# Seven products instead of eight for the last group of layer 2, and its h in a row ahead of y

## The chip, the cores and the metric

The kernel runs on one core of one Trainium2 chip. The metric is the device time of one execution in microseconds (us); the median of three runs stands for a kernel. A difference of about 0.2% of this kernel's time is what a measurement can tell from no change. The engines are TensorE (PE; its weight loads are PEld), VectorE (DVE), ScalarE (ACT), GpSimd (POOL), and SyncE (SP), which here only issues DMAs.

## What is computed

Random-feature attention and, on its result, two feed-forward layers without a bias, all in fp32 precision:

```python
x = attention(q, k, v, omega)        # reshaped to 2304 tokens x 512
h = x @ moe_w_in                     # 512 -> 2048
g = h - tanh(h)
x = g @ moe_w_out                    # 2048 -> 512
h = x @ moe2_w_in                    # layer 2, same sizes
g = h * (1.0 / (1.0 + exp(-1.702 * h)))
out = g @ moe2_w_out
```

TensorE multiplies fp32r numbers. Each operand is split into a rounded part (hi) and the rest (lo), and a product of two blocks is made as three matmuls (`PASSES`: hi hi, hi lo, lo hi), so that one block product of 128 x 128 weights by 384 tokens is three matmuls of 384 columns.

## The kernel before

Only layer 2 is touched. Its 2304 tokens are three blocks (`sb`) of 768, each of two halves of 384 (`TW`). Its 2048 features are eight pairs `j` of two 128-feature tiles. A group `n` is a pair of (block, j); there are `NG` = 24 groups, numbered 0 to 23. The first 16 belong to the blocks 0 and 1; groups 16 to 23 are the third block, with the pairs of `LAST` in order, so that group 23 has pair 2.

**h.** For a group h is a 2 x 2 block product (two feature tiles by two token halves), and it is made Strassen-Winograd fashion from seven products P1 to P7 instead of eight (`h_prod`, L906; each six matmuls, L916). They run in the order of `SLOTS` (P1, P7, P6, P4, P5, P2, P3), one in each of the seven slots `s` of a group's turn; the P2 in slot 5 is the next group's. P1, P6, P5, P3 add up in one PSUM bank (`a`), P7 and P4 in another (`c`), P2 in a third (`b`). Between the products other engines read the running sums and add them: `vec` (L1069 on) does in slot 0 `h_add` G11 (VectorE, reads bank a), in slot 1 the activation of G11 and the copy `s7` of bank c (ScalarE), in slot 2 the copy `s2` of bank a, in slot 3 `gsplit` of G11 and then `h_add` G21, in slot 4 the activation of G21 and `h_add` G22 (reads bank a), in slot 5 the activation of G22, in slot 6 `gsplit` of G21 and the activation of G12. So P6 may not write bank a until `h_add` G11 has read it, P5 not until `s2` has, and P3 not until `h_add` G22 has.

`gsplit` (L1027 on) makes the two parts of a g: a cast on ScalarE (L1035) and a subtraction (L1036), which is GpSimd's. The buffer for G21 (tag `g10`) exists once, those for G11 and G22 twice.

**y.** For groups 16 to 22 (`YG` <= n < `YE`, told by `yform`) y is made from seven products as well (`y_prod`, L984; `y_add`, L997). They need sums of w_out (`wfs`, loaded into `wos`) and the differences T1 to T4 of the g, which `forms` makes during the next group's turn: subtractions on GpSimd (L1040), then a cast on ScalarE (L1044) and a subtraction on GpSimd (L1045). The products write two PSUM tiles of two banks in turn; after each, VectorE adds the tile to an SBUF sum `yacc` (128 x 768, L997) before the next product writes that tile. Their order is `YP` (P3, P1, P2, P6, P7, P5, P4): in slots 1 to 6 of group n+1's turn stand P1 to P4 of group n, in slot 0 of the turn after that its P3. So h products of one group and y products of the one before it alternate on TensorE.

Group 23 is different: after the loop over its h, a last turn (n = 24) runs group 22's P3 and then eight plain chunks (`y_chunk`, L937, six matmuls each into one of four banks, 48 in all), each followed by a VectorE addition of 128 x 384 (L955; the last in two halves, L951) and a store.

The sums of w_out for the pairs 0 and 1 are made from the weights in SBUF at groups 2 and 3 (`late_ticks`), those for the pairs 3 to 7 when these weights are prepared. Pair 2 has none.

Each engine works off its instructions in the order in which the program issues them. Stores go through a list `later`, which `flush` issues on SP at the start of the next slot. All other DMAs of layer 2 are SP's too: in slot 0 of a group's turn stand the loads of the next group's w_in sums (`win`, in two pieces), of this group's w_out (`wout`) and, up to group 22, of its sums (`wos`).

Of the kernel before, what the change touches and what calls it, by code (L numbers as in the profile page):

```python
# [61 lines left out]
YG, YE = 2 * NPAIR, 3 * NPAIR - 1  # L62
YP = ("P3", "P1", "P2", "P6", "P7", "P5", "P4")
WID = dict(P1=0, P2=1, P7=2, P6=3, P5=4, P3=5, P4=6)
# [3 lines left out]
def body(ctx, tc, qT, kT, v, om, w1, w2, out):  # L68
# [393 lines left out]
    def out_sums(s, f1, f2):  # L462
        a11, a21, a12, a22 = f1[:, :256], f1[:, 256:], f2[:, :256], f2[:, 256:]
        for o, x, y, op in (
                (s[:, 0, :], a21, a22, ALU.add), (s[:, 2, :], a11, a21, ALU.subtract),
                (s[:, 1, :], s[:, 0, :], a11, ALU.subtract), (s[:, 3, :], a12, s[:, 1, :], ALU.subtract)):
            nc.gpsimd.tensor_tensor(out=o, in0=x, in1=y, op=op)

    def out_split(q, i, s, t):
        v = t.rearrange("p (a h c) -> p a h c", h=2, c=256)  # L470
        two(v[:, :, 0, :], v[:, :, 1, :], s[:, i:i + 2, :], nc.gpsimd)
        store(wfs[q, :, i * 512:(i + 2) * 512].rearrange("p (a h c) -> p a h c", h=2, c=256), v.bitcast(F32))


    def late_ticks(q):
        st = {}

        def whole():
            w = st["w"] = cv.tile([128, 2, 512], F32, tag="raw", name="wsum", bufs=2)
            nc.vector.tensor_tensor(  # L480
                out=w, in0=wout[q][:, :, 0, :].bitcast(F32), in1=wout[q][:, :, 1, :].bitcast(F32), op=ALU.add)

        def sums():
            st["s"] = ssum_tile((128, 4, 256))
            out_sums(st["s"], st["w"][:, 0, :], st["w"][:, 1, :])

        def part(i):
            out_split(q, i, st["s"], cv.tile([128, 2 * 512], F32R, tag="ye", name="stg", bufs=2))

        return [whole, sums, lambda: part(0), lambda: part(2)]  # L490

# [439 lines left out]
    def y_chunk(n, t, d):  # L931
        sb, j = GROUPS[n]
        yb = pt("hs" if n < NG - 1 else ("y2", "y0", "y3", "y1")[d])
        dst, k = yb[:, :TW], 0
        for f in range(2):
            for a, c in PASSES:
                nc.tensor.matmul(  # L937
                    dst, wout[j][:, f, a, d * 128:d * 128 + 128], gt[n, f, t][:, c, :], start=(k == 0), stop=(k == 5))
                k += 1
        first, last = (0, NPAIR - 1) if sb < 2 else (LAST[0], LAST[-1])  # L940
        if j == first and d % 2 == 0:
            yacc[sb, t, d // 2] = ya_tile("yacc")
        u = yacc[sb, t, d // 2][:, d % 2, :]
        if j == first:
            nc.vector.tensor_copy(out=u, in_=dst)
            return
        t0 = (2 * sb + t) * TW
        if n == NG - 1 and t == 1 and d == 3:
            for c, eng in ((0, nc.sync), (TW // 2, nc.scalar)):
                w = slice(c, c + TW // 2)  # L950
                nc.vector.tensor_tensor(out=u[:, w], in0=dst[:, w], in1=u[:, w], op=ALU.add)  # L951
                later.append((now[0], lambda eng=eng, w=w: eng.dma_start(
                    out=out[d, :, t0 + w.start:t0 + w.stop], in_=u[:, w])))
            return
        nc.vector.tensor_tensor(out=u, in0=dst, in1=u, op=ALU.add)  # L955
        if j == last:
            store(out[d, :, t0:t0 + TW], u)
# [14 lines left out]
    def y_prod(n, name):  # L972
        sb, j = GROUPS[n]
        i = "c" if name in ("P2", "P7", "P4") else "a"
        if name in ("P1", "P2", "P7"):
            ybank[n, i] = psb.tile([128, 2, 512], F32, tag="ya" if (i == "a") == (n % 2 == 0) else "yc", name="yb", bufs=1)
        dst = ybank[n, i]
# [4 lines left out]
        for d in range(2):  # L982
            for k, (a, c) in enumerate(PASSES):
                nc.tensor.matmul(  # L984
                    dst[:, d, :TW], w(a)[:, d * 128:d * 128 + 128], g[:, c, :],
                    start=(name in ("P1", "P2", "P7") and k == 0), stop=(k == 2), skip_group_check=True)

    def y_add(n, name):
        sb, j = GROUPS[n]
        src = ybank[n, "c" if name in ("P2", "P7", "P4") else "a"][:, :, :TW]  # L990
        h, t = dict(P1=(0, 0), P2=(0, 0), P3=(0, 1), P4=(1, 0), P5=(1, 1), P6=(1, 0), P7=(1, 1))[name]
        if n == YG and name in ("P1", "P6", "P7", "P3"):
# [4 lines left out]
        nc.vector.tensor_tensor(out=u, in0=src, in1=u, op=ALU.add)  # L997
# [29 lines left out]
    def gsplit(n, i):  # L1027
# [8 lines left out]
        nc.gpsimd.tensor_tensor(out=u[:, 1, :], in0=g, in1=u[:, 0, :].bitcast(F32), op=ALU.subtract)  # L1036
# [64 lines left out]

    do_y()
# [28 lines left out]
    for n in range(NG + 1):  # L1131
        sb, j = GROUPS[min(n, NG - 1)]
        for s in range(7):
# [6 lines left out]
            if n < NG or s < 2:  # L1140
                vec(n, s)
# [7 lines left out]
            if yform(m):  # L1149
                y_prod(m, YP[s])  # L1150
            if n == NG and s == 6:
                y_chunk(n - 1, 1, 3)
            if yform(m):
                y_add(m, YP[s])
                if m == YE - 1 and s == 0:
                    banks.close()
# [21 lines left out]
            q = n * 7 + s  # L1178
            if q in (16, 21):
# [33 lines left out]
            if n == 14:  # L1213
                if s == 0:
                    new_x2(2, 0)
                if SLOTS[s] != "P2":
                    new_x2(2, XID[SLOTS[s]])
    flush()
    assert not xticks and not later
# [46 lines left out]
```

## Time and profile before

| | us |
|---|---|
| median of 3 runs (lowest, highest) | 887.84 (887.63, 888.36) |
| the profiled execution | 888.12 |
| its span, first to last instruction | 886.0 |

| engine | busy us | share of the span | instructions |
|---|---|---|---|
| TensorE, matmuls | 880.8 | 99% | 5116 |
| VectorE | 617.5 | 70% | 956 |
| ScalarE | 582.6 | 66% | 1226 |
| GpSimd | 536.5 | 61% | 437 |

The chain that ended last is TensorE's to 99%. Times in the rows are us from the start of the span. A matmul's printed duration contains the time in which it drains; the distance of two starts tells what it costs in a row. In the stretch at the end of the kernel, the h products have L916, the seven-product y L984, the plain chunks L937.

### The profile page before, as it was taken

To read this page: it belongs to the slowest core of one execution; us is meant where nothing else is said; L and a number is where in the kernel's file an instruction comes from. 1 tells how busy PE (TensorE), PEld (TensorE's weight loads), DVE (VectorE), ACT (ScalarE), POOL (GpSimd) and SP (SyncE) were. 2 spreads that over 40 slices of the span, in tenths; PEclk is the share of its full clock that TensorE was granted. 3 is DMA by queue.
4 is the path that set the end of the run, shared out by engine and by line. 5 is a ranking of instruction groups with operands and counts; after the bars stand their busy time and mean duration, and the time that the engine had idled before them with its cause. 6 is when DMAs were issued, how large, how long until landed. Compare 5 with 4: busy or idle time off the path is not lost.

```text
span 886.0 us, 14390 instructions
## 1 busy us (share of the span) xinstructions
PE 880.8 (99%) x5116; PEld 806.2 (91%) x5116; DVE 617.5 (70%) x956; ACT 582.6 (66%) x1226; POOL 536.5 (61%) x437
## 2 busy tenths in 40 slices
PE   9999999999999999999999999999999999999998
PEld 7999988888898888888898899999999999999998
DVE  5889988766666655887777466477877775655555
ACT  7999988787777766777766645446565554544442
POOL 4555525656656565776866556537657565677774
PEclk9999999999999999999999999999999999999999
DMA  7888775033253341686471650824564224476752
GB/s 251 247 267 264 252 218 157 37 132 131 91 199 123 116 143 55 208 292 226 139 269 37 232 195 21 289 102 160 202 206 153 82 72 154 154 311 237 297 226 72
DMA packets 56071, 155.48 MB, mean 175 GB/s; under 512 B 6080, under 2 KB 12992, under 8 KB 52800
## 3 DMA queue, kind: packets, MB, share of 16 engines
q1 hardware_dynamic: 55712, 154.14, 50.3%
q8 instruction: 40, 0.66, 0.3%
q10 hardware_dynamic: 288, 0.43, 0.1%
q14 instruction: 31, 0.25, 0.1%
HBM read 106.32 MB, written 48.23 MB: 174 GB/s over the span
## 4 chain that ended last, share of the span: by engine, by line
PE 99%; ACT 1%; DVE 0%; issue 0%; DVEq 0%
PE y L418 22%; PE hs L380 22%; PE y L916 19%; PE hs L937 15%; PE yb L984 6%; PE y L220 3%; PE y L198 3%; PE y L134 2%; PE hs L165 2%; PE y L250 1%; PE y L937 1%; PE hs L916 1%; PE hs L168 1%; ACT kp L185 1%; PE y L216 1%; PE y L195 0%
## 5 line engine op out<-in xcount | busy, mean ns | idle before, releaser
L380 PE MATMUL hs<-xb,w 128*128 128x512 f32 (+1 forms) x960 | 209.1, 368 | 0.0
L380 PEld LDWEIGHTS hs<-xb,w 128*128 128x128 f32 x960 | 167.5, 189 | 30.0
L916 PE MATMUL y<-x,win 128*128 128x384 f32 x966 | 193.1, 334 | 0.0
L418 PE MATMUL y<-ghi,w 128*128 128x512 f32 (+1 forms) x640 | 192.4, 368 | 0.0
L394 POOL TENSOR_TENSOR glo<-wq,ghi 128x512 fp32r<-128x512 f32 x72 | 100.5, 1396 | 136.6 <-ACT ghi L392 135.0
L916 PEld LDWEIGHTS y<-x,win 128*128 128x128 f32 x966 | 169.8, 188 | 0.0
L410 DVE COPY_PREDICATED wq<-m,t 128x512 f32<-128x512 uint16 x72 | 88.5, 1230 | 104.6 <-POOL wq L408 102.8
L937 PE MATMUL hs<-g,wout 128*128 128x384 f32 x768 | 151.1, 334 | 0.0
L418 PEld LDWEIGHTS y<-ghi,w 128*128 128x128 f32 x640 | 116.6, 188 | 20.4 <-ACT ghi L392 0.4
L937 PEld LDWEIGHTS hs<-g,wout 128*128 128x128 f32 x768 | 134.8, 188 | 0.0
L418 PE MATMUL y<-glo,w 128*128 128x512 f32 (+1 forms) x320 | 117.8, 368 | 0.0
L1036 POOL TENSOR_TENSOR g<-sg,g 128x384 fp32r<-128x384 f32 x82 | 95.0, 1165 | 33.7 <-ACT g L1035 23.2
L408 POOL TENSOR_TENSOR wq<-wq,s 128x512 f32<-128x512 f32 x70 | 90.6, 1294 | 19.1 <-DVE wq L407 19.1
L955 DVE TENSOR_TENSOR yacc<-hs,yacc 128x384 f32<-128x384 f32 x112 | 61.4, 552 | 50.6 <-PE hs L937 49.8
L145 POOL PARTITION_ALL_REDUCE mq<-pq x32 | 62.6, 2002 | 53.0 <-ACT pq L143 53.0
L400 ACT ACTIVATE s<-hs 128x512 f32<-128x512 f32 x72 | 42.9, 596 | 60.0 <-PE hs L380 59.0
L418 PEld LDWEIGHTS y<-glo,w 128*128 128x128 f32 x320 | 60.3, 189 | 9.9
L997 DVE TENSOR_TENSOR yacc<-yb,yacc 128x768 f32<-128x768 f32 x45 | 43.1, 958 | 36.7 <-PE yb L984 36.5
L392 ACT CAST ghi<-wq 128x512 fp32r<-128x512 f32 x72 | 44.3, 615 | 29.1 <-DVE wq L410 29.0
L1023 ACT ACTIVATE sg<-y 128x384 f32<-128x384 f32 x55 | 27.0, 491 | 53.7 <-DVE y L1008 50.3
L331 DVE SCALAR_TENSOR_TENSOR raw<-raw 128x512 int32<-128x512 int32 x57 | 56.7, 995 | 2.0
L407 DVE SCALAR_TENSOR_TENSOR wq<-wq,hs 128x512 f32<-128x512 f32 x72 | 49.1, 682 | 12.6 <-ACT t L402 12.4
(153 smaller groups left out, 1518.0 us busy)
## 6 DMA issues: line engine op xcount, KB each, us to landing
raw<-w SPq DMA_DIRECT2D x57, 512.0 KB, 4.7
xb<-xs SPq DMA_DIRECT2D x24, 512.0 KB, 6.6
win<-wfi SPq DMA_DIRECT2D x9, 1280.0 KB, 6.8
wout<-wfo SPq DMA_DIRECT2D x9, 1024.0 KB, 8.3
wos<-wfs SPq DMA_DIRECT2D x7, 1024.0 KB, 8.8
xs<-xhl SPq DMA_DIRECT2D x12, 576.0 KB, 3.3
vt<-v SPq DMA_DIRECT2D x16, 325.0 KB, 4.2
wfs<-raw SPq DMA_DIRECT2D x10, 512.0 KB, 2.6
```

The lines of the kernel that those rows point to most:

```text
L145: nc.gpsimd.partition_all_reduce(mqs[i, j], pq[:, j * S:j * S + S], channels=128, reduce_op=bass.bass_isa.ReduceOp.max)
L331: nc.vector.scalar_tensor_tensor(out=c, in0=c, scalar=3, in1=z, op0=ALU.logical_shift_left, op1=ALU.bitwise_or)
L380: nc.tensor.matmul(h[:, j * n:j * n + n], w[:, 0, a, kt * 128:kt * 128 + 128], x[:, c, kt, :n], start=(k == 0), stop=(k == 11))
L394: nc.gpsimd.tensor_tensor(out=lo, in0=g, in1=hi.bitcast(F32), op=ALU.subtract)
L408: (nc.vector if si < 2 else nc.gpsimd).tensor_tensor(out=w, in0=w, in1=s, op=ALU.mult)
L410: nc.vector.copy_predicated(out=w, mask=m.bitcast(mybir.dt.uint16), data=t)
L418: nc.tensor.matmul(y[d][:, :n], w[:, 1, a, d * 128:d * 128 + 128], g[c][:, j * n:j * n + n], start=(first and j == 0 and k == 0), stop=(la ...
L916: nc.tensor.matmul(dst, w[:, WID[name], a, kt * 128:kt * 128 + 128], xt[:, kt, c, :], start=(first and k == 0), stop=(k == 5), skip_group_ ...
L937: nc.tensor.matmul(dst, wout[j][:, f, a, d * 128:d * 128 + 128], gt[n, f, t][:, c, :], start=(k == 0), stop=(k == 5))
L955: nc.vector.tensor_tensor(out=u, in0=dst, in1=u, op=ALU.add)
L984: nc.tensor.matmul(dst[:, d, :TW], w(a)[:, d * 128:d * 128 + 128], g[:, c, :], start=(name in ("P1", "P2", "P7") and k == 0), stop=(k == 2 ...
L1036: nc.gpsimd.tensor_tensor(out=u[:, 1, :], in0=g, in1=u[:, 0, :].bitcast(F32), op=ALU.subtract)
```

## The change

Group 23 makes y from seven products too (`YE` = 24), so `y_chunk` loses its special cases for the last group. Five things follow.

1. In group 23's turn the y products of group 22 are taken out (`LATE`), except P1 in slot 5; group 21's P3 stays in slot 0. So TensorE's order is: h P1, y P3 of 21, h P7, P6, P4, P5, y P1 of 22, h P3. In the last turn follow group 22's P2, P6, P7, P5, P4, P3 and group 23's P1; after the loop group 23's P2, P6, P7, P5, P4 and P3, the last in two halves by `d`, one VectorE addition for each and the very last in two halves of 192.
2. `vec` also runs in slots 0 to 5 of the last turn, for the forms of group 23.
3. In `gsplit` the subtraction for G11 and G21 of group 23 is VectorE's.
4. Group 23's products P1, P6, P5, P3 write the two h banks y0 and y2, with one VectorE addition of 128 x 384 for each; the others write one of the two tiles of the groups before, with an addition of 128 x 768. Stores go out after P2 and P4 (384 KB) and after P5 and P3 (192 KB and less).
5. The sums of w_out for pair 2 are made in groups 18 and 19 (`third_ticks`): two loads of 512 KB from DRAM in group 18's slot 0, two additions of 512 columns on VectorE in slots 5 and 6, four of 256 columns in group 19's slots 0 and 2, and in its slots 4 and 6 a cast on ScalarE, a subtraction on VectorE and a store of 512 KB. `load_wos` then runs for group 23 too.

```diff
-YG, YE = 2 * NPAIR, 3 * NPAIR - 1
+YG, YE = 2 * NPAIR, 3 * NPAIR
+LATE = {(NG - 1, s): (NG - 2, "P1" if s == 5 else None) for s in range(1, 7)}
+LATE.update({(NG, s): (NG - 2, (YP[2:] + YP[:1])[s]) for s in range(6)})
+LATE[NG, 6] = NG - 1, "P1"
...
+    def third_ticks(q):
...
+        def load():
+            for f in range(2):
+                t = st[f] = cv.tile([128, 2, 512], F32, tag="raw", name="wsum", bufs=2)
+                nc.sync.dma_start(out=t, in_=wfo[q, :, f * 1024:(f + 1) * 1024].rearrange("p (h c) -> p h c", h=2))
...
+        def whole(f):
...
+            nc.vector.tensor_tensor(out=st["w"][:, f, :], in0=st[f][:, 0, :], in1=st[f][:, 1, :], op=ALU.add)
...
+            out_sums(st["s"], st["w"][:, 0, :], st["w"][:, 1, :], nc.vector, part)
...
+            out_split(q, i, st["s"], cv.tile([128, 2 * 512], F32R, tag="ye", name="stg", bufs=2), nc.vector)
+
+        return {0: load, 5: lambda: whole(0), 6: lambda: whole(1), 7: lambda: sums(0), 9: lambda: sums(1),
+                11: lambda: part(0), 13: lambda: part(2)}
...
-    def y_prod(n, name):
+    def y_prod(n, name, ds=(0, 1)):
...
+            if n == NG - 1 and i == "a":
+                ybank[n, i] = [pt(f"y{2 * d}")[:, :TW] for d in range(2)]
...
+        for d in ds:
+            ends = (0, TW // 2, TW) if name == "P3" and d else (0, TW)
+            for a, b in zip(ends, ends[1:]):
+                nc.vector.tensor_tensor(out=u[:, d, a:b], in0=src[d][:, a:b], in1=u[:, d, a:b], op=ALU.add)
...
         nc.scalar.copy(out=u[:, 0, :], in_=g)
-        nc.gpsimd.tensor_tensor(out=u[:, 1, :], in0=g, in1=u[:, 0, :].bitcast(F32), op=ALU.subtract)
+        (nc.vector if n == NG - 1 and not t else nc.gpsimd).tensor_tensor(
+            out=u[:, 1, :], in0=g, in1=u[:, 0, :].bitcast(F32), op=ALU.subtract)
...
-            if n < NG or s < 2:
+            if n < NG or s < 6:
                 vec(n, s)
...
+            m, name = LATE.get((n, s), (m, YP[s]))
+            if name and yform(m):
+                y_prod(m, name)
+                y_add(m, name)
...
+    for name in YP[2:] + YP[:1]:
+        for ds in ((0,), (1,)) if name == "P3" else ((0, 1),):
+            flush()
+            y_prod(NG - 1, name, ds)
+            y_add(NG - 1, name, ds)
     flush()
+    banks.close()
```

## Rows read from the trace of the kernel before

**Rows 1.** The page: busy time, share of the span and instructions of each engine.
```profile
PE 880.8 (99%) x5116; PEld 806.2 (91%) x5116; DVE 617.5 (70%) x956; ACT 582.6 (66%) x1226; POOL 536.5 (61%) x437
```
**Rows 2.** The chain that ended last, its end: start us, us, what.
```profile
874.17 8.34 PE y L937 x48
...
882.53 0.36 DVE yacc L951
```
**Rows 3.** Windows: stretch, busy us (instructions) by engine, granted clock, DMA share, GB/s.
```profile
0.00:5.00 5.00, 3.50 (x8) 1.78 (x8) 0.80 (x4) 1.28 (x1) 0.19 (x4) 1.00 0.59 202
...
801.20:815.76 14.56, 14.56 (x86) 14.56 (x86) 8.39 (x10) 6.32 (x14) 10.90 (x12) 1.00 0.69 271
...
859.43:874.01 14.58, 14.58 (x86) 14.56 (x85) 9.24 (x11) 6.76 (x15) 11.12 (x13) 1.00 0.19 73
```
**Rows 4.** Timeline of TensorE, group 23's h P1 and P7: start us, us, engine, line.
```profile
859.43 1.20 PE L916 MATMUL y<-x,win 128*128 128x384 f32 x6
...
861.51 1.20 PE L916 MATMUL y<-x,win 128*128 128x384 f32 x6
```
**Rows 5.** Timeline of SP: the load of a group's w_out sums.
```profile
788.91 0.32 SPq L967 DMA_DIRECT2D wos<-wfs  x1
```
**Rows 6.** DMA issues, 780 to 886 us: KB each, median us to landing.
```profile
wos<-wfs SPq DMA_DIRECT2D x5, 1024.0 KB, 8.9
...
out<-yacc SPq DMA_DIRECT2D x7, 192.0 KB, 1.9
```
**Rows 7.** VectorE's groups by form: shapes, count, busy us, mean ns, idle before.
```profile
L460 DVE TENSOR_TENSOR wout<-raw,wout 128x512 fp32r<-128x512 f32 x10 | 8.6, 858 | 0.0
...
L480 DVE TENSOR_TENSOR wsum<-wout 128x1024 f32<-128x1024 f32 x2 | 2.8, 1382 | 0.0
```
**Rows 8.** Timeline of VectorE in group 23's turn: a y addition, an h_add.
```profile
861.71 0.96 DVE L997 TENSOR_TENSOR yacc<-yb,yacc 128x768 f32<-128x768 f32 x1 [0.40 <-PE yb L984]
...
868.99 0.56 DVE L1008 TENSOR_TENSOR hx<-y,s 128x384 f32<-128x384 f32 x1
```
**Rows 9.** The chain at the kernel's start: start us, us, what.
```profile
0.96 0.50 DVE warm L101
1.50 3.03 PE y L628 x4
```
**Rows 10.** Timeline of GpSimd in group 23's turn: T2's split, T3, T3's split.
```profile
863.72 1.01 POOL L1045 TENSOR_TENSOR fT<-T,fT 128x384 fp32r<-128x384 f32 x1 [2.13 <-ACT fT L1044]
864.70 1.01 POOL L1040 TENSOR_TENSOR T<-sg,sgb 128x384 f32<-128x384 f32 x1
866.33 1.02 POOL L1045 TENSOR_TENSOR fT<-T,fT 128x384 fp32r<-128x384 f32 x1 [0.62 <-ACT fT L1044]
```
**Rows 11.** Timeline of ScalarE in group 23's turn: the casts of T3 and G11.
```profile
865.74 0.51 ACT L1044 CAST fT<-T 128x384 fp32r<-128x384 f32 x1 [0.42 <-POOL T L1040]
866.15 0.51 ACT L1035 CAST g<-sg 128x384 fp32r<-128x384 f32 x1
```
**Rows 12.** Tile xi: VectorE's SBUF subtractions, duration ns min/median/max, first and last start.
```profile
L460 DVE TENSOR_TENSOR x<-xi,x x21: 543/552/1353, 452.6 to 763.6; 128x384 fp32r<-128x384 f32 x21
```
**Rows 13.** Timeline of VectorE, 747 to 758 us: subtractions between SBUF operands.
```profile
747.79 0.94 DVE L609 TENSOR_TENSOR xi<-xi 128x384 f32<-128x384 f32 x1
...
752.42 0.55 DVE L460 TENSOR_TENSOR x<-xi,x 128x384 fp32r<-128x384 f32 x1
752.89 0.55 DVE L609 TENSOR_TENSOR xi<-xi 128x384 f32<-128x384 f32 x1
...
757.46 0.90 DVE L460 TENSOR_TENSOR x<-xi,x 128x384 fp32r<-128x384 f32 x1
```
**Rows 14.** Timeline of GpSimd in the same stretch.
```profile
747.30 1.02 POOL L460 TENSOR_TENSOR x<-xi,x 128x384 fp32r<-128x384 f32 x1 [1.13 <-ACT x L459]
...
757.91 1.32 POOL L460 TENSOR_TENSOR x<-xi,x 128x384 fp32r<-128x384 f32 x1
```
**Rows 15.** The page's costliest groups: GpSimd's splits of g, mean ns of one.
```profile
L1036 POOL TENSOR_TENSOR g<-sg,g 128x384 fp32r<-128x384 f32 x82 | 95.0, 1165 | 33.7 <-ACT g L1035 23.2 <-issue 7.9 <-PE hs L937 1.4
```

## What the change was predicted to do

> **What bounds the kernel now.** I read the shares and the chain first. TensorE is busy for 880.8 of the 886.0 us span [rows 1], and the end of the chain is 48 matmuls without a gap and one VectorE addition behind them [rows 2]. By stage, a group in the row of seven-product groups and the last stretch of h both have TensorE busy in all of their time, at a granted clock of 1.00, that is 2.4 GHz [rows 3]. So fewer matmuls save time only if none starts to wait; the busy shares of the other engines matter only through the moment at which each answers TensorE. That has to be read in the order of the last 25 us. The profiled execution took 888.12 us for its span of 886.0; the median of the runs is 887.84. I work out a difference on the span and add it to the median.
>
> **What the change removes.** A product is six 384-column matmuls and takes 1.04 us from start to start (two from 859.43 to 861.51 [rows 4]); the printed 1.20 contains 0.16 of drain. Group 23's 48 y matmuls become 7 products of 6, that is 42: **-1.04 us**. On GpSimd three splits of group 23 go (G11 and G21 to VectorE, G12 altogether), and eight forms and splits come; they sit beside other work unless a product waits for them, see below.
>
> **What it adds in the third block.** In groups 18 and 19: two 512 KB loads, two 512-column sums, four 256-column sums and two 512-column subtractions on VectorE, two casts on ScalarE, two 512 KB stores. A group's loads are issued within some 3.5 us, the last at 788.91 for the group that starts at 786.64 [rows 5], and this one lands 8.9 us later [rows 6], in a group of 14.56 us [rows 3]; the 1 MB more is moved in the idle rest. The stores wait on SP ahead of group 20's load of w_in, which is due five slots later. From like instructions (1.38 us for two sums of 512 at once, 0.86 for a subtraction, and 0.69 as half of the 1.38 for each sum of 256 as a bound [rows 7]) VectorE gets some 5.9 us in two groups, each of which uses 8.39 of 14.56 us there [rows 3]. A y product's bank is needed again three products (3.12 us) after its end and its addition takes 0.20 + 0.96 [rows 8], so 1.9 us are spare; no single tick is longer than that. I take **0**; if GpSimd holds each of them up, two additions come late, and it costs up to 0.6 by my estimate from these spares.
>
> **What it moves: the row of h.** Group 23's P1, P7, P6, P4, P5 now stand with only group 21's P3 (after P1) and group 22's P1 (after P5) between them, and P3 follows. P3 accumulates into the bank that h_add G22 reads, so it waits for VectorE. I follow the queues, each instruction starting when its engine is free and its operand there, with the hand-overs of the rows: a product's last 1.04 us plus 0.20 to VectorE or ScalarE (860.48 + 1.04 to 861.71 [rows 8]), and 0.04 from VectorE to TensorE (0.96 + 0.50 to 1.50 [rows 9]).
> P1 starts at 859.43, P3 of group 21 1.04 later and P7 at 861.51, as before [rows 4]; P6, P4, P5 and group 22's P1 follow at 1.04 each, and TensorE is ready for P3 at 866.71. After P7 ScalarE casts T2, GpSimd splits T2 at 863.72 and forms T3 until 865.71 [rows 10]; ScalarE's next instructions are the cast of T3 (865.74) and, behind it, the cast of G11 (866.15 to 866.67) [rows 11]. None of these moves, because they hang on P7 and on GpSimd's order. But before, the split of G11 was GpSimd's, and VectorE was free for h_add G21 and G22. Now the subtraction stands on VectorE **ahead** of both. It starts at 866.70, while GpSimd splits T3 (866.33 to 867.35 [rows 10]).
> Such a subtraction takes 0.55 us at the median, at most 1.35 [rows 12]. A VectorE instruction on SBUF operands that started inside a GpSimd instruction took 0.94 us and ended 0.41 after it (748.73 against 748.32); beside none it took 0.55 [rows 13, 14]. So G11 ends at 867.35 + 0.41 = 867.76.
> The two h_adds follow (0.56 each [rows 8], the second 0.47 behind the first, as the pair at 752.42 and 752.89 in [rows 13]), each starting 0.09 before the last ends, as such a pair does: G22 ends at 868.71, and P3 starts at 868.75. **+2.04 us** (1.60 with a subtraction of 0.55, 2.4 with one of 1.35).
> The Trainium skill ("SBUF — State Buffer", section "SBUF: two separate sides") says that a VectorE operation with two SBUF inputs and a GpSimd operation exclude each other, the later one fully blocked. Taken to the letter, by an estimate, the whole 0.55 us would follow GpSimd's end, 0.14 more than rows 13 and 14 have, and the sum below would be 0.28 higher; the rows decide.
>
> **The first y product that is late.** G21 of group 23 goes into the one buffer that group 22's P2 reads, and P2 now follows P3: it ends at 870.83. The cast starts 0.20 later and ends at 871.54. The subtraction behind it meets GpSimd again. GpSimd's split of T1 began under G11's subtraction; an instruction in that place took 1.32 and ended 0.87 after VectorE's (757.91 under 757.46 [rows 13, 14]), so it ends at 868.63; then T4, its cast and its split bring the split of group 22's G22 to 871.21, and it ends at 872.23. So the subtraction of G21 ends at 872.64. Behind it stands the addition of P2: 872.55 to 873.51. P7 starts the same bank anew and waits for it until 873.55, while P6 has ended at 871.87: **+1.68 us** (1.20 with both subtractions at 0.55, 2.0 with both at 1.35).
>
> **The rest of the row of y.** With no h between, a bank is needed 1.04 us after its product's end, and the answer takes 0.20 + 0.96 + 0.04 = 1.20. One stall of 0.16 pays for two products; following the banks, it falls on P4 of group 22 and on P2, P7 and P4 of group 23: **+0.64**. At the end VectorE's last addition starts not 0.17 us behind TensorE's last matmul (882.36 without its drain, 882.53 [rows 2]) but behind P4's addition and a half of P3's: 0.20 + 0.87 + 0.47 - 1.04 = 0.50, **+0.33**. The last two 96 KB stores now follow 384 and 192 KB instead of 192 every 1.04 us; a 192 KB store lands in 1.9 us [rows 6] and nothing shows such a pile, so I take 0, up to 0.5. GpSimd's chain for group 23 (T1 from 872.2, T4's split done near 882.4) is ahead of P4, which starts near 883.6, by 1.2 us.
>
> **Sum.** -1.04 + 2.04 + 1.68 + 0.64 + 0.33 = +3.65 us: 887.84 + 3.65 = **891.5** (in the profiled execution 888.12 + 3.65 = 891.8). With the lower bounds, 1.60 and 1.20, it is +2.7 (890.5); with every upper one, 2.4 and 2.0 and 0.6 and 0.5, it is +5.4 (893.3).
>
> **Rivals.**
> *A, no conflict on SBUF.* Both subtractions take 0.55: the lower bounds above, 890.5. For it: the median row; against: GpSimd is at work almost without a break when each starts.
> *B, the queues answer in time.* If VectorE were done with h_add G22 before group 22's P1 ends (866.71), and with the addition of P2 before P6 ends, only the small stalls would stay: 887.84 - 1.04 + 0.64 + 0.33 = 887.8, not slower. It decides at one point, whether the cast of G11 stands behind T3's on ScalarE as it does now [rows 11]; the program's order leaves that, so T3 would have to come 2 us earlier, and GpSimd waits for P7 there. Little speaks for it.
> *C, GpSimd becomes the bound.* Its 384-column instructions took 1.02 in this stretch [rows 10] but 1.165 at the mean of the whole run [rows 15]. Ten of groups 22 and 23 at 0.15 more bring T4's split 1.5 us later, beyond the 1.2 that it has, and the h row's GpSimd steps 0.3: 0.3 to 1.1 more, 892.3.
> *D, the clock.* The granted clock is 1.00 in each row, also in the first 5 us, where TensorE idled for 1.5 us [rows 3, 9]; no row has a longer stop. If one of 2.04 us brought the level of 1.2 GHz, thirteen products would take 2.08 instead of 1.04: +13.5, near 905. The Trainium skill ("TensorE: Matmul & The Clock Gate", "Part 1: The HAM clock gate") tells of such a fall to half after idling; no run here shows one so far.
>
> **Chances.** Forecast 0.62, A 0.14, B 0.12, C 0.09, D 0.03. A difference of 0.2% (1.8 us) is about what a measurement of this kernel can tell from no change; slower by that begins at 889.6. Forecast, A, C and D are slower, 0.88; I take 0.05 off for stalls that come out below A's: slower 0.83, within 0.2% 0.14, faster 0.03 (B with more saved than the matmuls). The range leaves out B and D; it reaches from 0.6 below A, since each hand-over is read from one row, to the upper sum: **889.9 to 893.3**.
>
> **What would show it.** In the profile of the changed kernel: TensorE's waits, of which before has almost none, should name h_add G22 (about 2.0 us, once) and the addition of group 22's P2 (about 1.7, once), then four of about 0.16; the subtraction of G11 on VectorE should take about 1.06 us; groups 18 to 20 should keep 14.56 us each. The forecast is wrong if P3 of h starts within a few tenths of group 22's P1, if TensorE's waits name GpSimd's splits, or if the groups of the third block grow.

## The result

The changed kernel takes 893.9 us at the median of six runs (892.4 to 894.25), the kernel before 888.09 beside it (six runs, 887.63 to 888.37): a ratio of 1.006, 95% interval 1.0049 to 1.0071. It is slower, by 5.8 us, and lies above the predicted range. The profiled execution took 893.73 for its span of 891.9; before it was 888.12 for 886.0. So 5.90 us went into the span (and 0.29 less lay outside it), where the prediction had 3.65.

The page of after answers [rows 1]: VectorE and GpSimd work somewhat more, TensorE still fills 99%.

```profile
span 891.9 us, 14413 instructions
PE 882.2 (99%) x5110; PEld 805.5 (90%) x5110; DVE 626.5 (70%) x969; ACT 585.3 (66%) x1231; POOL 544.2 (61%) x442
```

TensorE's timeline from group 23's h P1 on (start, us, then engine, line, shapes; in brackets the idle time before and its releaser; h products have L943 now, y products L1009). Before, 22 products or chunks stood here 1.04 us apart [rows 2, 4].

```profile
860.18 1.20 PE L943 MATMUL y<-x,win 128*128 128x384 f32 x6
861.23 1.20 PE L1009 MATMUL yb<-g,wos 128*128 128x384 f32 x6
862.26 4.32 PE L943 MATMUL y<-x,win 128*128 128x384 f32 x24
866.42 1.20 PE L1009 MATMUL yb<-g,wout 128*128 128x384 f32 x6
869.48 1.31 PE L943 MATMUL y<-x,win 128*128 128x384 f32 x6 [1.85 <-DVE hx L1047]
870.62 1.20 PE L1009 MATMUL yb<-g,wout 128*128 128x384 f32 x6
871.66 1.20 PE L1009 MATMUL yb<-fT,wos 128*128 128x384 f32 x6
874.36 2.35 PE L1009 MATMUL yb<-fT,wos 128*128 128x384 f32 x12 [1.49 <-DVE yacc L1025]
876.80 1.28 PE L1009 MATMUL yb<-fT,wout 128*128 128x384 f32 x6
877.92 1.24 PE L1009 MATMUL yb<-g,wos 128*128 128x384 f32 x6
879.00 1.21 PE L1009 MATMUL y<-g,wout 128*128 128x384 f32 x6
880.30 1.28 PE L1009 MATMUL yb<-g,wout 128*128 128x384 f32 x6
881.42 1.21 PE L1009 MATMUL y<-fT,wos 128*128 128x384 f32 x6
...
886.26 1.21 PE L1009 MATMUL y<-g,wos 128*128 128x384 f32 x6
```

Two long gaps stand out, with the two releasers that the prediction named. TensorE is ready for h P3 at 866.42 + 1.04 = 867.46 and starts it at 869.48, 2.02 us later (bracketed as 1.85, since the row before is drawn with its drain); it is ready for P7 at 872.70 and starts it at 874.36, 1.66 later. Behind them a product comes after 1.04 us no more: two take 2.44 (874.36 to 876.80), then the steps are 1.12, 1.08, 1.30, 1.12, and on to the end 1.30 and 1.12 in turn.

VectorE's timeline over the first gap answers [rows 8], GpSimd's [rows 10]:

```profile
867.51 0.98 DVE L1075 TENSOR_TENSOR g<-sg,g 128x384 fp32r<-128x384 f32 x1 [4.09 <-ACT g L1074]
868.41 0.55 DVE L1047 TENSOR_TENSOR y<-y,s 128x384 f32<-128x384 f32 x1
868.88 0.54 DVE L1047 TENSOR_TENSOR hx<-y,s 128x384 f32<-128x384 f32 x1
```
```profile
867.07 2.27 POOL L1085 TENSOR_TENSOR fT<-T,fT 128x384 fp32r<-128x384 f32 x2 [0.62 <-ACT fT L1084]
```

The subtraction of G11 begins inside T3's split, takes 0.98 instead of 0.55, and both h_adds stand behind it. The end of the span shows in the chain (start, us, what):

```profile
885.14 1.29 PE yb L1009 x6
886.43 0.02 issue
886.46 0.96 DVE yacc L1025
887.41 0.47 DVE yacc L1032
887.88 0.26 DVEq L1309
```

The 5.90 us of the span then come from four places.

| stretch | before | after | difference |
|---|---|---|---|
| start of the span to group 23's h P1 | 859.43 | 860.18 | +0.75 |
| h P1 to the end of TensorE's last matmul, without drain | 22.93 | 27.12 | +4.19 |
| from there to the start of VectorE's addition for the last half product (before: the last chunk) | 0.17 | 0.49 | +0.32 |
| from there to the end of the span (the last stores) | 3.47 | 4.11 | +0.64 |

The 4.19 are 21 products instead of 22 (-1.04), less 0.05 that before lost too, plus 2.02, plus 1.66, plus 0.10 for h P3 (1.14 instead of 1.04), plus 1.50 for the unsteady steps behind. The first line, +0.75, is no effect of the change: it arises in the kernel's first 8 us, which the change does not touch. The chain at the start answers [rows 9], first before, then after:

```profile
4.53 0.43 PE hs L161 x2
4.96 1.62 PE y L165 x16
```
```profile
4.53 0.71 PE hs L164 x2
5.25 2.06 PE y L168 x16
```

In the fourteen traces of this case the 16 matmuls took from 1.14 to 2.06 us, whatever the edit (1.14 and 2.01 in two kernels that differ only from group 22 on, 2.06 also in the first experiment, where group 23 is as before); so below a kernel is measured by "h P1 to TensorE's end" (22.93 before, 27.12 after), which this start does not enter.

### The profile page after: what moved, and what is told of

The parts are those of the page before. It is cut to its first block, busy times and chain, and to the rows that moved or that the text cites. A ratio compares the mean times of both kernels' runs of the same rounds, so it can differ in the third digit from the quotient of the medians.

```text
span 891.9 us, 14413 instructions
## 1 busy us (share of the span) xinstructions
PE 882.2 (99%) x5110; PEld 805.5 (90%) x5110; DVE 626.5 (70%) x969; ACT 585.3 (66%) x1231; POOL 544.2 (61%) x442
## 4 chain that ended last, share of the span: by engine, by line
PE 97%; ACT 1%; DVE 1%; POOL 1%; issue 0%; DVEq 0%; POOLq 0%; ACTq 0%
PE y L421 22%; PE hs L383 22%; PE y L943 18%; PE hs L964 15%; PE yb L1009 6%; PE y L223 3%; PE y L201 3%; PE y L137 2%; PE hs L168 2%; PE y L253 1%; PE hs L943 1%; PE hs L171 1%; ACT kp L188 1%; PE y L219 0%; PE y L198 0%
## 5 line engine op out<-in xcount | busy, mean ns | idle before, releaser
L943 PE MATMUL y<-x,win 128*128 128x384 f32 x966 | 192.8, 334 | 1.8 <-DVE hx L1047 1.8
L943 PEld LDWEIGHTS y<-x,win 128*128 128x128 f32 x966 | 169.7, 188 | 2.2 <-DVE hx L1047 2.2
L1075 POOL TENSOR_TENSOR g<-sg,g 128x384 fp32r<-128x384 f32 x79 | 92.4, 1177 | 34.0 <-ACT g L1074 24.0
L1025 DVE TENSOR_TENSOR yacc<-yb,yacc 128x768 f32<-128x768 f32 x48 | 45.8, 955 | 29.4 <-PE yb L1009 29.2
```

The lines of the kernel that those rows point to most:

```text
L943: nc.tensor.matmul(dst, w[:, WID[name], a, kt * 128:kt * 128 + 128], xt[:, kt, c, :], start=(first and k == 0), stop=(k == 5), skip_group_ ...
L1075: (nc.vector if n == NG - 1 and not t else nc.gpsimd).tensor_tensor(out=u[:, 1, :], in0=g, in1=u[:, 0, :].bitcast(F32), op=ALU.subtract)
```

## The experiments

Theory: the moved subtractions stand on VectorE ahead of what TensorE waits for; the rest is small waits of VectorE's round trip. Rivals: the third block costs something; GpSimd is the bound in any order; the clock; the last stores. Each kernel has 5 to 11 runs. Ratios are to the kernel before, run beside it (medians of 888.27, 888.35 and 888.58 us in the three sets).

### Is it the third block?

Before, with the third block's sums made and stored, and read by nobody (`third_ticks` added, `YE` left as it was).

```diff
+            if n == NG - 6 and s == 0:
+                t3 = third_ticks(LAST[-1])
+            if 0 <= q - 7 * (NG - 6) in t3:
+                t3[q - 7 * (NG - 6)]()
```

> The kernel before with one part of the change alone: the sums of w_out for pair 2 are made in groups 18 and 19 and stored, and nobody reads them; group 23 stays as it was. Theory (the whole loss is made behind group 23's first product): time as before, ratio 1.000 within 0.0007, groups 18 to 20 keep 14.56 us each. Rival (the third block's work pushes TensorE or lengthens the start): 0.5 to 0.8 us more than before, the 0.75 us by which group 23 began later in the changed kernel's trace.

Measured: 887.69 us, 0.9994 [0.9985, 1.0003]; h P1 to TensorE's end 22.92. The windows of groups 18 and 19 (stretch, busy us (instructions) of TensorE, weight loads, VectorE, ScalarE, GpSimd, granted clock, DMA share, GB/s) show why:

```profile
786.70:801.26 14.56, 14.56 (x86) 14.56 (x85) 8.82 (x11) 6.32 (x15) 10.93 (x12) 1.00 0.89 342
801.26:815.82 14.56, 14.56 (x86) 14.56 (x85) 12.29 (x17) 6.68 (x16) 11.19 (x11) 1.00 0.69 271
```

VectorE is busy for 12.29 of 14.56 us (8.39 before [rows 3]), DMA for 0.89, and TensorE misses nothing. The third block costs nothing.

### Is it where the subtractions stand?

Three kernels, each the changed one with one edit. First: both subtractions back on GpSimd.

```diff
-        (nc.vector if n == NG - 1 and not t else nc.gpsimd).tensor_tensor(
-            out=u[:, 1, :], in0=g, in1=u[:, 0, :].bitcast(F32), op=ALU.subtract)
+        nc.gpsimd.tensor_tensor(out=u[:, 1, :], in0=g, in1=u[:, 0, :].bitcast(F32), op=ALU.subtract)
```

> The changed kernel with one part undone: GpSimd makes the subtractions for G11 and G21 of group 23, as before. Theory (a chain of queues): TensorE's wait of 1.8 us for h_add G22 vanishes and the wait for the addition of group 22's P2 falls from 1.5 us to 0.25, but GpSimd's two instructions more come back as waits for its splits of T2, T3 and T4 of group 23 (0.6, 1.5 and 1.4 us); from group 23's first product to TensorE's end 26.6 us (27.1 in the changed kernel, 22.9 before), so 0.3 to 0.7 us less than the changed kernel. Rival (the subtractions on VectorE are the whole of the loss): 3.5 us less than the changed kernel, and no wait for GpSimd.

Measured: 893.08 us, 1.0053 [1.0041, 1.0066]; h P1 to TensorE's end 26.36. Both long gaps are gone, and other ones have come. TensorE's waits from 859 us on (engine, line, waited for: us in all, times, longest):

```profile
PE yb L1009 <- POOL fT L1084: 1.3, 2, 0.6
PE yb L1009 <- ACT fT L1083: 0.7, 2, 0.4
```

P7 and P4 of group 23 now wait for GpSimd's forms and their casts, which the two subtractions push back. So the move to VectorE cost TensorE two long waits, and the move back returns only 0.76 us of them (27.12 to 26.36).

Second: VectorE keeps them, G11's behind h_add G22 and G21's behind the addition of P2.

```diff
             elif s == 3:
-                gsplit(n, G11)
+                if n < NG - 1:
+                    gsplit(n, G11)
...
                 h_add(n, G22, a, sv.pop((n, "s7")))
+                if n == NG - 1:
+                    gsplit(n, G11)
...
+                if (m, name) == (NG - 2, "P2"):
+                    gsplit(NG - 1, G21)
```

> The changed kernel with VectorE's order mended and nothing else: G11's split stands behind h_add G22, G21's behind the addition of group 22's P2. Theory: TensorE's wait for h_add G22 vanishes; a wait for the addition of P1 (1.0 us) and one for that of P6 (1.7 us) come instead, because each subtraction still stands ahead of some addition and waits for a cast that stands behind T3's and T4's: 26.1 us from group 23's first product to the end, 1.0 us less than the changed kernel. Rival (only the order of two instructions on VectorE is wrong): 3.7 us less.

Measured: 892.01 us, 1.0042 [1.0029, 1.0056]; 26.01. h P3 follows without a gap, which shows that the place of G11's subtraction made that gap. But TensorE waits later on the additions that stand behind the two subtractions, P6 on that of P1 and P5 on that of P6:

```profile
869.52 2.44 PE L1009 MATMUL yb<-fT,wos 128*128 128x384 f32 x12 [0.67 <-DVE yacc L1025]
873.49 1.28 PE L1009 MATMUL yb<-fT,wos 128*128 128x384 f32 x6 [1.53 <-DVE yacc L1025]
```

Third: the subtractions stay where the change puts them; the forms of groups 22 and 23 come in the order T1, T2, T3, split of T2, T4, split of T3, splits of T1 and T4, so that T3's cast, and G11's behind it on ScalarE, come earlier.

```diff
+        if n >= NG - 2:
+            if s == 0:
+                tform(n, "T1", G12, G11)
+                tform(n, "T2", G22, "T1")
+            elif s == 1:
+                tform(n, "T3", G22, G12)
+                tsplit(n, "T2")
...
```

> The changed kernel with another order of the forms of groups 22 and 23 on GpSimd: T1, T2, T3, T2's split, T4, then the other splits, so that it does not stand idle while ScalarE casts. The subtractions stay on VectorE ahead of the h_adds. Theory (the casts behind T3's are late because GpSimd is): the wait for h_add G22 falls from 1.8 to 0.5 us, that for the addition of P2 to 1.3; 25.1 us from group 23's first product to the end, 2.0 us less than the changed kernel. Rival (VectorE is late by its own load, not by GpSimd): no change.

Measured: 891.33 us, 1.0034 [1.0021, 1.0046]; 25.25. The wait on h_add G22 shrinks from 1.85 to 0.23, that on P2's addition from 1.49 to 1.24. This is rival B's condition met in part, for the first wait: T3's cast starts 4.73 us behind h P1 (864.98) instead of 6.30 (866.48), and the wait is nearly gone. Here VectorE's subtraction of G21 began while GpSimd stood idle (871.01, in its pause from 870.74 to 871.44) and took 0.56; in the changed kernel, beside a GpSimd instruction, it took 0.81.

### The changed kernel again, and the tight row

> The changed kernel once more, beside the next three. Theory: of the 5.9 us by which its span was longer, 0.75 were there before group 23's first product and come from the kernel's first 8 us, which no line of the change touches, so they come and go; 5.1 to 5.3 us over the kernel before if the start is alike, TensorE 27.1 us from group 23's first product to its end. Rival (the start is slower because of the change): 5.8 again, and again some 0.7 us lost in the first 8 us.

Measured: 893.95 us, 1.0063 [1.005, 1.0075]; 27.08. The difference repeats, 5.6 us instead of the 5.1 to 5.3 expected. Three of its five runs (893.95 to 894.12) show the lower clock that the next experiment tells of; the two others take 893.37 and 893.49, 5.0 and 5.1 more than the kernel before.

Then the additions of 128 x 768 in halves, with four banks of their own for group 23:

```diff
-            if n == NG - 1 and i == "a":
-                ybank[n, i] = [pt(f"y{2 * d}")[:, :TW] for d in range(2)]
+            if n == NG - 1:
+                ybank[n, i] = [pt(f"y{2 * d + (i == 'c')}")[:, :TW] for d in range(2)]
...
-                ybank[n, i] = t[:, :, :TW]
+                ybank[n, i] = t[:, :, :TW] if n < NG - 2 else [t[:, d, :TW] for d in range(2)]
```

> The changed kernel with one thing else: in the row of y the additions are made for each half (128 x 384, one bank) and group 23 has banks of its own, so that a bank is given back half a product earlier. The order of the queues stays. Theory (the four small waits of 0.25 with the slow first matmuls behind them are the turn of one bank): all four vanish, the wait for h_add G22 stays at 1.8 to 2.1, that for the addition of P2 falls to 1.0 to 1.2; 25.3 us from group 23's first product to TensorE's end, 1.8 less than the changed kernel. Rival (VectorE has too much to do in the row of y): the waits stay, since halves take VectorE longer in sum.

Measured: 892.21 us, 1.0045 [1.0033, 1.0058]. In group 23 it does what it should: its seven products take 7.28 us, 1.04 each. Yet h P1 to TensorE's end is 27.10, not the 25.3 expected. The windows (columns as above) and TensorE's timeline tell where it went:

```profile
868.00:870.00 2.00, 1.01 (x5) 1.01 (x6) 1.87 (x5) 0.63 (x2) 1.83 (x2) 0.97 0.03 8
870.00:872.00 2.00, 2.00 (x8) 2.00 (x8) 0.00 (x0) 1.20 (x3) 1.55 (x2) 0.50 0.00 0
872.00:874.00 2.00, 1.96 (x8) 1.64 (x6) 0.82 (x2) 0.91 (x2) 0.87 (x2) 0.68 0.00 0
```
```profile
868.99 1.56 PE L943 MATMUL y<-x,win 128*128 128x384 f32 x6 [1.84 <-DVE hx L1047]
870.35 2.12 PE L1009 MATMUL yb<-g,wout 128*128 128x384 f32 x6
872.27 1.68 PE L1009 MATMUL yb<-fT,wos 128*128 128x384 f32 x6
874.82 2.35 PE L1009 MATMUL yb<-fT,wos 128*128 128x384 f32 x12 [0.86 <-DVE yacc L1032]
877.33 1.28 PE L1009 MATMUL yb<-fT,wout 128*128 128x384 f32 x6 [0.16 <-DVE yacc L1032]
```

A granted clock of 0.50, that is 1.2 GHz, just after TensorE's wait of 1.84 us: h P3 took 1.36 and P2 1.92 instead of 1.04 each, 1.2 us lost. Most of the other 0.6 is group 22's: P7 starts 1.51 after P6 would have ended at the full clock (872.27 + 1.04 to 874.82; 1.0 to 1.2 were expected), and P7 and P5 take 2.51 instead of 2.08. The profiled execution of the changed kernel shows 1.00 in all these windows, so this is something that some executions have. The mean clock of each run tells which: of the 21 runs of kernels with the long wait unfilled (the changed kernel, the changed kernel again, this one, and the one without a store below) 15 have 0.997 or 0.998; of the 70 runs of all other experiments none is below 0.999, nor is any run of the kernel before beside them. In the changed kernel's six runs the three with 0.997 or 0.998 average 894.15 us, the others 893.01, 1.1 us less; when it ran again, 894.01 and 893.43, 0.6 less. The start, which differs by up to 0.9 us, is in these times, so the traces are the better price.

### Is it the clock, and is it the stores?

Unread matmuls in the two waits, nine ahead of h P3 and seven ahead of P7:

```diff
+    def fill(k):
+        t = pt("y0")[:, :TW]
+        for _ in range(k):
+            nc.tensor.matmul(t, wout[GROUPS[NG - 2][1]][:, 0, 0, :128], gf[NG - 2, "B11"][:, 0, :], start=True, stop=True)
...
+            if (n, s) == (NG - 1, 6):
+                fill(9)
...
+            if (n, s) == (NG, 2):
+                fill(7)
```

> The changed kernel with matmuls that nobody reads in its two long waits: nine of 384 columns (1.56 us) ahead of group 23's P3 of h, seven (1.21 us) ahead of group 22's P7 of y. Theory (in part of the executions of the changed kernel the granted clock falls to 1.2 GHz for some 3 us after the wait of 1.85 us, as the trace of the kernel with additions by halves shows): every run shows a mean clock of 1.000 and the time falls by 0.3 to 0.8 us against the changed kernel, though TensorE does more. Rival (the recorded clock is noise, or the waits cost nothing but their length): no change, or a few tenths more, with clocks of 0.997 as before.

Measured: 893.38 us, 1.0054 [1.0042, 1.0067], 0.5 below the changed kernel's median, and no mean clock below 0.999. h P1 to TensorE's end is 27.13: with the wait filled, everything else stays as it was, and the slower clock does not come. The clocks show this; the 0.5 us alone would not, since the two intervals overlap.

The changed kernel without the 384 KB store behind P4 (output features 256 to 511 of the last block's first 384 tokens are not written):

```diff
-            if done:
+            if done and name != "P4":
```

> The changed kernel without the store behind group 23's P4 (384 KB): the output features 256 to 511 of the last block's first 384 tokens are not written. Theory (the last two 96 KB stores land 0.8 us later than before because 384 and 192 KB stand ahead of them): they land in 1.6 to 1.9 us again, 0.5 to 0.8 us less than the changed kernel, TensorE unchanged. Rival (the later end is the time that VectorE's last additions take): they land as late as in the changed kernel.

Measured: 893.32 us, 1.0056 [1.0044, 1.0069], 0.6 below the changed kernel. Its DMA issues from 878 us on (KB each, median us to landing), and behind them those of the changed kernel:

```profile
out<-yacc SPq DMA_DIRECT2D x1, 96.0 KB, 1.8
out<-yacc ACTq DMA_DIRECT2D x1, 96.0 KB, 1.9
```
```profile
out<-yacc SPq DMA_DIRECT2D x1, 96.0 KB, 2.6
out<-yacc ACTq DMA_DIRECT2D x1, 96.0 KB, 2.4
```

Before, these two landed in 1.6 and 1.7 us. The changed kernel's last stores queue behind P4's 384 KB, and that is most of the 0.64 at the end of the span: without that store it is 3.57 us from the last addition's start to the end (887.93 to 891.5), against 4.11 with it and 3.47 before. The median does not tell this apart from noise, and the expectation that TensorE stays as it was did not hold: four of this kernel's five runs show the lower clock, its profiled one among them: 0.74 in the window 868 to 870 us, 0.50 from 870 to 872. There h P1 to TensorE's end is 28.27, 1.15 more than in the changed kernel's profiled execution, which has no such fall.

### The row undone, and the parts combined

The changed kernel without the row (h of 23 and y of 22 alternate as before; seven products and the third block stay):

```diff
-LATE = {(NG - 1, s): (NG - 2, "P1" if s == 5 else None) for s in range(1, 7)}
-LATE.update({(NG, s): (NG - 2, (YP[2:] + YP[:1])[s]) for s in range(6)})
-LATE[NG, 6] = NG - 1, "P1"
+LATE = {}
...
-    for name in YP[2:] + YP[:1]:
+    for name in YP[:1]:
```

> The changed kernel without the row: group 23 makes y from seven products and its sums are made in the third block as in the change, the subtractions stay on VectorE, but group 22's y products alternate with group 23's h as before, and group 23's P1 to P3 follow. Theory (the loss is the row's): no wait for h_add G22 and none for the addition of group 22's P2; TensorE waits for GpSimd's splits of T3 and T4 instead (about 1.5 and 1.4 us), 25.4 us from group 23's first product to TensorE's end against 27.1: 1.5 to 2.3 us less than the changed kernel, 3 us over the kernel before. Rival (the row saves what it is there for, and only its details are wrong): as slow as the changed kernel or slower.

Measured: 891.36 us, 1.0032 [1.002, 1.0044]; 25.25. Neither of the long waits is there; P7 and P4 of group 23 wait for GpSimd's forms (1.3 us) and ScalarE's casts (0.6). So the row does have a purpose: it gives GpSimd time for group 23's forms. In the changed kernel no product waits for them.

Combined: the subtractions on GpSimd, the forms in the new order, the additions in halves.

> The changed kernel with the three causes taken away: GpSimd makes the subtractions again, the forms of groups 22 and 23 stand in the other order, the additions are made by halves. Theory: one wait is left, 0.4 us for T3's split; 22.4 us from group 23's first product to TensorE's end (22.9 before), the last stores land 0.5 to 0.8 us later after the last addition than before: within 0.5 us of the kernel before, whichever side. Rival (something in the row is missed): 1 us or more over the kernel before.

Measured: 887.44 us, 0.9992 [0.9983, 1.0001]; 22.69, with 0.85 left over 21 times 1.04: in group 22, whose halves still share one tile, P6 takes a step of 1.37, P7 and P5 2.49 together.

The same, but with VectorE's subtractions placed behind h_add G22 and P2's addition:

> As the last, but with the subtractions on VectorE, G11's behind h_add G22 and G21's behind the addition of group 22's P2. Theory: no wait of TensorE in the row; 21.9 us from group 23's first product to TensorE's end, that is the 1.04 us of the six matmuls less than before; with the later landing of the last stores 0.0 to 0.6 us under the kernel before. Rival: the subtractions still hold up additions, as in the kernel with only VectorE's order mended: a wait of 1 us or more, and over the kernel before.

Measured: 889.17 us, 1.0011 [1.0002, 1.002]; 23.84, where 21.9 was expected. VectorE's timeline and GpSimd's:

```profile
870.17 1.36 DVE L1075 TENSOR_TENSOR g<-sgb,g 128x384 fp32r<-128x384 f32 x1
871.46 1.94 DVE L1032 TENSOR_TENSOR yacc<-yb,yacc 128x384 f32<-128x384 f32 x4
```
```profile
870.10 1.01 POOL L1080 TENSOR_TENSOR T<-sgb,sg 128x384 f32<-128x384 f32 x1
871.19 1.19 POOL L1080 TENSOR_TENSOR T<-sg,T 128x384 f32<-128x384 f32 x1
```

The subtraction began 0.07 after a GpSimd instruction and lasted until 0.42 after its end, and the additions behind it came late: a wait of 0.93 on TensorE. So even in this place a subtraction holds up an addition that a bank waits for, while GpSimd works beside it; the expectation had missed that.

Last, the combination on GpSimd with a PSUM tile of its own for each half of group 22's sums too:

```diff
+            elif n == NG - 2:
+                ybank[n, i] = [psb.tile([128, 512], F32, tag=f"y{i}{d}", name="yb", bufs=1)[:, :TW] for d in range(2)]
...
+            if (n, s) == (NG - 1, 5):
+                banks.close()
+                psb = pool("psumc", banks, space=bass.MemoryType.PSUM, reuse_waits="tile")
```

> The kernel with the three causes taken away (subtractions on GpSimd, the forms in the other order, additions by halves), and beside it a PSUM tile of its own for each half of group 22's sums, whose products still waited 0.2 to 0.4 us twice for both halves' additions. Theory: these two waits vanish, one of some 0.4 us for GpSimd's split of T3 is left; 22.3 us from group 23's first product to TensorE's end (22.9 before), the last stores land 0.3 us later than before: 0.5 to 1.2 us under the kernel before. Rival: GpSimd gives back all of it, as fast as the last.

Measured: 887.45 us (11 runs, 886.79 to 887.72), 0.9989 [0.9981, 0.9998]; 22.25. Its median is below both kernels', that of the one before by 1.1 us; that is less than the 0.2% a measurement of a few runs can tell, but the interval of these leaves out 1. In TensorE's timeline one step of about 0.4 in group 23 (876.31 to 879.84, 3.53 for P6, P7 and P5) is all that is left over 1.04 each. The chain names what it waits for, GpSimd's split of T3, which ends at 877.78, as expected:

```profile
876.31 3.69 PE L1011 MATMUL y<-fT,wos 128*128 128x384 f32 x18
879.84 1.20 PE L1011 MATMUL y<-fT,wout 128*128 128x384 f32 x6
```
```profile
876.80 0.98 POOL fT L1086
877.82 2.19 PE y L1011 x11
```

## Where the prediction was right, and where wrong

**Right.** The direction and the two mechanisms. The wait for h_add G22 is 2.02 us (2.04 predicted), that for P2's addition 1.66 (1.68), each in its place. The subtraction of G11 took 0.98 (1.06) and ended 0.41 after the GpSimd instruction beside it; the experiment that moves it behind the h_add removes its gap, the one that moves it to GpSimd removes both. Six matmuls less give 1.04 us. The third block costs 0, as its own experiment shows. The last addition comes 0.32 later (0.33). So rival A fell, and rival B's condition, T3 earlier on ScalarE, was not met in the change; the reordered forms came near it for the first wait and took most of it away. The prediction's own steps give 1.53 to 2.33 and 1.16 to 1.96 for the bounds of the two waits, up to 0.08 less than it wrote; its range moves by 0.1 at most.

The Trainium skill ("SBUF — State Buffer", section "SBUF: two separate sides") says that the later of the two is blocked for the whole instruction of the other. The traces agree that it is held up; but the subtraction ends 0.41 us after GpSimd's in the changed kernel and 0.42 after it in the rows of the kernel with VectorE's subtractions in their better place, less than the 0.55 that it takes alone, so the measured rows [rows 13, 14] stay the better price.

**Wrong: the size of the rest.** The sum said +3.65 for a span that grew by 5.90. Three steps account for the 2.25.

- *The rest of the row of y*, 0.64 for four waits of 0.16. It cost 1.50, and h P3's own 0.10 besides. The waits fall on the four products named, P4 of group 22 and P2, P7 and P4 of group 23, but are 0.26 each (1.04 in all): the addition starts 0.20 after its product and takes 0.96, as predicted, but TensorE starts 0.14 after its end (881.62 + 0.96 = 882.58, next start 882.72), not 0.04. That 0.04 was read at the hand-over of a small memset [rows 9], not at one like this. After the 128 x 384 h_add it was 0.05 (869.43 to 869.48). It is not the size: behind the 128 x 384 halves of a y addition the combination on GpSimd has 0.15 again (868.76 + 0.55 = 869.31 to 869.46, the first two rows below, VectorE's and TensorE's). What sets the two kinds of hand-over apart stays open. The other 0.46 is six products that take 0.04 to 0.10 longer than 1.04, all but one directly behind a wait; the prediction had no such term. In the changed kernel's trace, taken matmul by matmul, it is mostly the first matmul behind a wait, 0.25 to the next start instead of 0.17 (the last two rows, P2 of group 23), and 0.28 in h P3. Why is open too.

```profile
868.76 0.55 DVE L1032 TENSOR_TENSOR yacc<-yb,yacc 128x384 f32<-128x384 f32 x1
869.46 2.35 PE L1009 MATMUL yb<-fT,wos 128*128 128x384 f32 x12 [0.16 <-DVE yacc L1032]
```
```profile
880.30 0.41 PE L1009 MATMUL yb<-g,wout 128*128 128x384 f32 x1
880.55 0.51 PE L1009 MATMUL yb<-g,wout 128*128 128x384 f32 x2
```

- *The last stores*, taken at 0 and at most 0.5: 0.64. The mechanism that the prediction named, a pile behind 384 KB, is the one that the kernel without that store shows: 0.54 of it goes.
- *The start of the kernel*, not in the sum: +0.75 in the one execution. It is a draw that each execution makes anew, and no work of the change.

The sum: 1.50 + 0.10 - 0.64 = 0.96, plus 0.64, plus 0.75, less 0.05 that before lost too, less 0.05 by which the three right terms came out smaller, is 2.25.

**Rival D** was drawn too coarsely. The prediction let the clock fall for thirteen products or not at all, and gave it 0.03. By the mean clock it falls in 15 of 21 runs, and the two traces that have it show 1.2 GHz for some 3 us: 1.15 and 1.2 us lost. It enters the median of 893.9, since half of the six runs have it. Together the median comes out: 5.15 of the change in the span (4.19 + 0.32 + 0.64), less 0.29 outside it, are 4.9 without the fall, 5.6 with the slow start of the profiled execution, and 6.0 with the fall; measured 5.8, the mean of the profiled run (893.73) and one with the fall (894.07). The Trainium skill ("TensorE: Matmul & The Clock Gate", "Part 1: The HAM clock gate") tells of a fall to half after idling. The windows with 0.50 behind a single wait of 1.85 us agree with it in kind, and so do the runs with the wait filled, none below 0.999; it speaks of longer idling than this wait, and here the measurement decides.

**Rival C** did not hold in the change itself, where GpSimd's splits are in time because TensorE is late. With the forms in their old order it is what came next where GpSimd got the subtractions or the row was undone: 1.9 to 2.0 us of waits on the forms and their casts. With the forms in the new order GpSimd took the subtractions for 0.4 us of such waits (the last experiment). The prediction's reserve of 1.2 us for them was counted with the late TensorE.

## What to carry to other kernels

An instruction that is moved to an engine with time to spare is priced by what stands behind it in that engine's queue: here two 0.55 us subtractions on an engine that is busy 70% cost TensorE 3.7 us, since each stood in front of the release of a bank. The engine that they leave is not a free place either: moved back, they returned 0.8 us, until GpSimd's forms stood in a better order. When a row of products has only one product's time between a bank's end and its next use, read the whole round trip from a hand-over of the same kind on the same engines, 1.30 us here and not 1.20; with a bank for each half group 23's row held, at 1.04 us a product. And look at what the last stores queue behind: 384 KB just ahead of them cost 0.5 us here.

## What was not expected of the hardware

- A single wait of TensorE of about 1.85 us was followed, in two traces, by some 3 us at a granted clock of 0.50, and by the mean clock in 15 of 21 runs. The five runs of the kernel whose longest wait was 1.53 us show none.
- The kernel's first matmuls differ by execution: the same 16 took 1.14 to 2.06 us, though the windows there show a granted clock of 1.00 in every trace. Why is open.
- VectorE's hand-over to TensorE took 0.14 to 0.15 us behind a y addition, of 128 x 768 or of 128 x 384, and 0.05 behind an h_add of 128 x 384.
- The first matmul behind such a wait took 0.25 to 0.28 us to the next start instead of 0.17, at a granted clock of 1.00.
- A VectorE subtraction that begins 0.07 us after a GpSimd one lasts 1.36 us instead of 0.55, and the next GpSimd one 1.19 instead of 1.01.
